# RWKV5 attention and a gated mixture of experts on one core: VectorE operands in PSUM, tables, routing and own terms divided differently

## The chip, the cores and the metric

The kernel runs on one core of a Trainium2 chip. The metric is the device time of one execution in microseconds (us). The core has a matrix engine (TensorE, PE in the profile; PEld is its weight load), three engines for elementwise work (VectorE or DVE, ScalarE or ACT, GpSimd or POOL), and SyncE (SP), which here issues loads and stores. The engines read a large on-chip memory, SBUF, with 128 partitions. TensorE writes into PSUM, a smaller memory of eight banks of 512 float32 values per partition, which the other engines can read and write too.

## The reference, cut to what matters

All values are float32. Attention has 4 batches, 8 heads, 768 positions and 48 values per head. It keeps, for every batch and head, a 48x48 state that decays by `w`; the token's own term is weighted by `u` instead:

```python
for t in range(S):
    kt, vt, rt = (k[:, :, t], v[:, :, t], r[:, :, t])
    cur = np.einsum('bhd,bhe->bhde', u[None] * kt, vt)
    y[:, :, t] = np.einsum('bhd,bhde->bhe', rt, state + cur)
    state = w[None, :, :, None] * state + np.einsum('bhd,bhe->bhde', kt, vt)
```

Its output becomes 3072 rows of 384 values. A gate picks a group of four and in it an expert of four for each row; the weight is the product of both softmax values, each with 1e-9 added to its sum. The expert is `relu(x @ w1) @ w2` with 1024 hidden values:

```python
g_idx = np.argmax(x @ w_group, axis=1)
# for the rows of group g: e_idx = argmax(xg @ w_expert[g])
h = np.maximum(xg[mask_e] @ w1[g, e], 0.0)
out[tok_idx] = (g_w * e_w)[:, None] * (h @ w2[g, e])
```

## The kernel before, in words

**Attention in chunks.** The 768 positions are cut into six chunks of 128. A chunk of one batch is a tile, `n = 4c + b`, 24 in all; two tiles make a pair `g` whose k, r and v are loaded together. With a table of powers of w by position (`T1`) and one of inverse powers (`T2`), scaled r and k (`rp`, `kp`) turn the recurrence within a chunk into matrix products. The scores of a tile (`PA`, L369) are copied below the diagonal into a matrix `am` (L373). Its diagonal is filled with the own terms `du` (sum of r·k·u, L354) by a predicated copy whose mask is the identity `id_ps` in PSUM (L380). The output `Y` is the state `R` times r (L394, from chunk 1 on) plus `am` times v (L401); the new state is `U` (L411) plus the old one, times the power of a whole chunk, `WL` (L419, L420; in chunk 0 L416 alone).

**Gate and routing.** ACT copies `Y` to `yT` (L406). A product with the gate weights `gwp` (L426), a copy `lT` (L431), and a second small product with `sel` (L447) give 20 gate values of each row, which ACT copies to `lg` (L449). `yT` is turned into rows (L436) and copied to `xt` (L441). When a chunk's four tiles are there, VectorE picks the experts (L135 to L149), PE adds up the rows already given to each expert (L153, L156), VectorE works out places and gate weights (L164 to L184), and POOL writes the rows with four indirect DMAs (L188) to the memory region of their expert. After chunk 3 (iteration 18) the two experts with most rows so far are chosen, and their weights are loaded ahead.

**The order.** One loop, `for s in range(-3, 25)`, is pipelined over tiles. Iteration s holds, in this order: the scores of tile s+1; the values of tile s, with U and R; every second time the sum `du`, for the pair of tiles s+2 and s+3, and each time the diagonal of tile s+2; the gate parts of tile s-1; the turning of k of tile s+3 (L359 on PE, L361 on ACT); the rows of tile s-1; the turning of r of tile s+3; the gate sum of tile s-1; and parts of the routing. The orders of PE, ACT, VectorE and SP are those of the program text (a manual schedule); POOL's instructions may be moved by the scheduler. Each engine takes its instructions in order, so an instruction that waits holds up what is behind it. k and r are turned through the same PSUM bank `KR`, so the transposes of r wait until ACT has copied k's. POOL makes `dg` (L337, L338), `kp` and `rp` (L348, L349), four products of 128x768 for each pair.

**Start.** Before the loop VectorE makes the powers `pw` and a reciprocal of all 512 columns, `iw` (L261). Both are transposed into `KR` and `RW` and copied to the tables by VectorE (L267). VectorE makes the first pair's `kp` (L345), POOL its `rp`. POOL clears the pads of `kp`, `rp` (L251) and the three `am` (L277). The small constants (start rows, `desc`, `bias16`, `sel`) are made by VectorE (L314 to L329) behind iotas of POOL.

**Experts.** Sixteen slots follow, in order of row counts. For each, rows are fetched (`xg`), turned, multiplied with w1 (L650) and w2 (L662), and written to the output with indirect DMAs (L674). The change does not touch them.

Of the kernel before, what the change touches and what calls it, by code (L numbers as in the profile page):

```python
# [8 lines left out]
FP32 = mybir.dt.float32  # L9
# [17 lines left out]
def kernel(  # L27
# [75 lines left out]
    WL = cst([P, HC], "WL")  # L103
# [28 lines left out]
    def route_choice(tl, L, T, sums):  # L132
# [3 lines left out]
        key = tl([P, T, NA, Eg], "key")  # L136
# [6 lines left out]
        oh = tl([P, T, NA, Eg], "oh")  # L143
        nc.vector.tensor_tensor(out=oh, in0=key, in1=spread(kx, 3, Eg), op=OP.is_equal)
        ohe = tl([P, T, G, Eg], "ohe")
        nc.vector.tensor_mul(ohe, oh[:, :, 1:NA, :], spread(oh[:, :, 0, :], 3, Eg))
        ohf = ohe.rearrange("p i g e -> p i (g e)")
        for i in range(T):
            nc.vector.tensor_add(sums[:, i + 1, :], sums[:, i, :], ohf[:, i, :])  # L149
        return mx, oh, ohe  # L150
# [10 lines left out]
    def route_place(tl, pre, ohe, T):  # L161
        ohf = ohe.rearrange("p i g e -> p i (g e)")
        at = tl([P, T, GE], "at")
        nc.vector.tensor_mul(at, pre.rearrange("p (i e) -> p i e", e=GE), ohf)  # L164
        place = tl([P, T], "place")
        nc.vector.reduce_sum(out=place, in_=at, axis=AX)
        place_i = tl([P, T], "place_i", U32)
        nc.vector.tensor_copy(place_i, place)
        return place_i

    def route_gate(tl, L, mx, oh, xt, T):
        NA = 1 + G
        ex = tl([P, T, NA, Eg], "ex")
        nc.vector.tensor_sub(ex, L, spread(mx, 3, Eg))
        nc.scalar.activation(ex, ex, AF.Exp)
        sx = tl([P, T, NA], "sx")
        nc.vector.reduce_sum(out=sx, in_=ex, axis=AX)
        nc.vector.tensor_scalar(out=sx, in0=sx, scalar1=1e-9, scalar2=None, op0=OP.add)
        gg = tl([P, T, G], "gg")
        nc.vector.tensor_mul(gg, sx[:, :, 1:NA], oh[:, :, 0, :])  # L180
        se = tl([P, T], "se")
        nc.vector.reduce_sum(out=se, in_=gg, axis=AX)
        nc.vector.tensor_mul(se, se, sx[:, :, 0])
        nc.vector.reciprocal(xt[:, :, :, Q_GATE], spread(se, 2, NQ))  # L184
# [11 lines left out]
    with ExitStack() as rec:  # L196
# [14 lines left out]
        id_ps = U[:, 256 : 256 + P]  # L211
        lT_ps = MS[:, 0:P]
        lg_ps = MS[:, P : P + NL]
        pre_ps = MS[:, 192 : 192 + B * GE]
        cnt_ps = MS[:, 192 + B * GE : 192 + B * GE + GE]

        R = [ring.tile([P, HC, D], FP32, name=f"R_{b}") for b in range(B)]
        NKP, NRP, NAM = 4, 3, 3
# [15 lines left out]
        wraw = ring.tile([P, HC], FP32, name="wraw")  # L234
        nc.vector.memset(wraw, 0.9)
        wv = w.rearrange("(hc e) d -> e d hc", e=2)
        for e, queue in enumerate((nc.sync, nc.scalar)):
            queue.dma_start(out=wraw[DP * e : DP * e + D, :], in_=wv[e])
        raw[0, "k"] = load(k, 0, "kt", 2)
        raw[0, "r"] = load(r, 0, "rt", 2)  # L240
# [9 lines left out]
        for t in kp + rp:  # L250
            nc.gpsimd.memset(t[:, :, :, D:DP], 0.0)  # L251

        pw = ring.tile([P, HC, P + 1], FP32, name="pw")
        iw = ring.tile([P, HC, P], FP32, name="iw")
        nc.vector.tensor_scalar(out=wcol, in0=wraw, scalar1=W_LEAST, scalar2=W_MOST, op0=OP.max, op1=OP.min)
        nc.vector.memset(pw[:, :, 0:1], 1.0)
        nc.vector.tensor_copy(pw[:, :, 1], wcol)
        for i in range(7):
            n = 1 << i
            nc.vector.tensor_mul(pw[:, :, 1 + n : 1 + 2 * n], pw[:, :, 1 : 1 + n], spread(pw[:, :, n], 2, n))  # L260
        nc.vector.reciprocal(iw, pw[:, :, 1 : P + 1])  # L261
        nc.vector.tensor_copy(WL, pw[:, :, P])

        def table(src, dst, bank):
            for hc in range(HC):
                nc.tensor.transpose(bank[:, hc, :], src[:, hc, 0:P], ident)
            nc.vector.tensor_copy(dst, bank.rearrange("p hc (e x) -> p (hc e) x", e=2)[:, :, 0:D])  # L267

        table(iw, T2, KR)
        table(pw, T1, RW)  # L270

        nc.vector.memset(Y, 0.0)
        nc.vector.memset(U, 0.0)
        nc.vector.tensor_copy(id_ps, ident)
        nc.vector.memset(ones, 1.0)
        for t in am:
            nc.gpsimd.memset(t, 0.0)  # L277

        nc.gpsimd.memset(gwp, 0.0)
        wg = moe_w_group.rearrange("(h d) g -> d h g", d=D)  # L280
        for m in range(2):
            rows = slice(DP * m, DP * m + D)
            nh = H - 2 * m
            nc.scalar.dma_start(out=gwp[rows, 0:nh, 0:G], in_=wg[:, 2 * m : H, :])
            for g in range(G):
                we = moe_w_expert[g].rearrange("(h d) x -> d h x", d=D)
                nc.scalar.dma_start(out=gwp[rows, 0:nh, G + Eg * g : G + Eg * (g + 1)], in_=we[:, 2 * m : H, :])

        def consts():
            nc.gpsimd.iota(iota_f, pattern=[[1, P]], base=0, channel_multiplier=0, allow_small_or_imprecise_dtypes=True)  # L290
            nc.gpsimd.iota(tok4, pattern=[[NQ * P, NCH], [NQ * S, B], [1, NQ]], base=0, channel_multiplier=NQ)
            nc.gpsimd.iota(
                region, pattern=[[RG, GE]], base=0, channel_multiplier=0, allow_small_or_imprecise_dtypes=True
            )
            for i, n in enumerate(SLOTS):
# [7 lines left out]
        FILL = ((P, P + 48), (P + 48, P + 96), (P + 96, 256))  # L303
        zeros = ring.tile([48, XW], FP32, name="zeros")
        nc.vector.memset(zeros, 0.0)

        def fill(i):
            lo, hi = FILL[i]
# [660 lines left out]
```

## Time and profile before

| what | us |
|---|---|
| median of 14 runs | 475.77 (474.52 to 477.61) |
| the profiled execution | 475.31, of it the profiled span 473.6 |
| start, to the first steady scores | 35.3 |
| chunk 0, iterations 0 to 3 | 21.2 |
| iterations 4 to 19 | 108.9 |
| last iterations, routing, first rows | 38.0 |
| experts | 270.2 |
| granted TensorE clock, mean | 0.953 |

The stages are cut at the starts of L369 for tile 1 (35.28), tile 5 (56.52) and tile 21 (165.40), and at the first product of the experts (203.38). In a line of the profile's timeline the first number is the start in us from the span's beginning and the second the duration; then come engine, line and operation, output and inputs, partitions x elements, and how many instructions the row stands for. In brackets stands how long the engine stood idle before, and what ended that. A busy engine is one that works on an instruction, even where that instruction proceeds slowly.

### The profile page before, as it was taken

To read this page: it belongs to the slowest core of one execution; us is meant where nothing else is said; L and a number is where in the kernel's file an instruction comes from. 1 tells how busy PE (TensorE), PEld (TensorE's weight loads), DVE (VectorE), ACT (ScalarE), POOL (GpSimd) and SP (SyncE) were. 2 spreads that over 40 slices of the span, in tenths; PEclk is the share of its full clock that TensorE was granted. 3 is DMA by queue.
4 is the path that set the end of the run, shared out by engine and by line. 5 is a ranking of instruction groups with operands and counts; after the bars stand their busy time and mean duration, and the time that the engine had idled before them with its cause. 6 is when DMAs were issued, how large, how long until landed. Compare 5 with 4: busy or idle time off the path is not lost.

```text
span 473.6 us, 9117 instructions
## 1 busy us (share of the span) xinstructions
PE 400.4 (85%) x3510; PEld 374.1 (79%) x3510; DVE 202.7 (43%) x377; ACT 154.4 (33%) x311; POOL 222.1 (47%) x223
## 2 busy tenths in 40 slices
PE   0359998789779896089999999999999999999990
PEld 0237877567568774079999999999999999999990
DVE  7896687998998874310121022022102211222100
ACT  0213444324334433213333423424342334144410
POOL 6798543967766303400532542452254335432444
PEclk9999999899899898579999999999999999999995
DMA  8899995647621299328698789779888988899100
GB/s 142 109 201 189 192 191 125 109 77 170 101 52 53 67 309 291 112 53 204 181 248 223 201 228 278 182 227 274 215 216 229 290 192 246 248 277 247 56 22 27
DMA packets 124018, 83.53 MB, mean 176 GB/s; under 512 B 96564, under 2 KB 115140, under 8 KB 123968
## 3 DMA queue, kind: packets, MB, share of 16 engines
q1 hardware_dynamic: 115136, 73.08, 65.8%
q0 software_dynamic: 4960, 9.55, 6.6%
q10 hardware_dynamic: 3872, 0.25, 0.6%
q8 instruction: 29, 0.48, 0.4%
q14 instruction: 21, 0.17, 0.1%
HBM read 70.11 MB, written 13.29 MB: 176 GB/s over the span
## 4 chain that ended last, share of the span: by engine, by line
issue 42%; DVE 18%; PE 18%; POOL 16%; DMA 4%; ACT 2%; POOLq 1%; DVEq 0%; ACTq 0%
POOL out_dram L674 15%; PE Y L401 4%; PE PA L369 4%; DVE R L420 3%; PE KR L359 3%; DMA out_dram<-yt,idn 3%; DVE am L380 2%; PE Y L394 2%; DVE am L373 2%; ACT kT L361 2%; PE U L411 1%; PE MS L426 1%; DVE du L354 1%; DVE key L138 1%; DVE kp L345 1%
## 5 line engine op out<-in xcount | busy, mean ns | idle before, releaser
L674 POOL DMA_INDIRECT out_dram<-yt,idn x107 | 104.1, 973 | 167.5 <-DVE yt L672 125.6
L650 PE MATMUL ph<-xe,w 128*128 128x200 f32 (+12 forms) x768 | 132.2, 332 | 9.9 <-DMA xg<-x_sorted 9.9
L650 PEld LDWEIGHTS ph<-xe,w 128*128 128x128 f32 x768 | 129.5, 192 | 10.2 <-issue 9.9
L662 PE MATMUL po<-hT,w2p 128*128 128x200 f32 (+12 forms) x768 | 130.4, 330 | 0.0
L662 PEld LDWEIGHTS po<-hT,w2p 128*128 128x128 f32 x768 | 128.1, 190 | 0.0
L671 DVE STREAM_TRANSPOSE yt<-yT 128x672 f32<-128x672 f32 (+1 forms) x16 | 13.6, 847 | 215.4 <-ACT yT L665 215.4
L655 ACT ACTIVATE hT<-ph 128x416 f32<-128x416 f32 (+12 forms) x64 | 32.0, 500 | 102.8 <-PE ph L650 102.8
L640 ACT COPY w2p<-w 128x1024 f32<-128x1024 f32 x48 | 47.1, 1048 | 9.3 <-DMA x_sorted<-xt,place_i 9.3
L188 POOL DMA_INDIRECT x_sorted<-xt,place_i x24 | 23.8, 991 | 53.2 <-ACT lg L449 18.8
L665 ACT COPY yT<-po 128x208 f32<-128x208 f32 (+12 forms) x48 | 15.6, 324 | 69.1 <-PE po L662 67.2
L373 DVE COPY_PREDICATED am<-later,PA 128x1024 f32<-128x1024 int32 x24 | 31.4, 1308 | 11.8 <-PE PA L369 11.3
L369 PE MATMUL PA<-rT,kT 48*128 48x128 f32 x384 | 30.0, 299 | 7.0 <-DVE am L373 7.0
L369 PEld LDWEIGHTS PA<-rT,kT 48*128 48x128 f32 x384 | 25.1, 200 | 8.8 <-DVE am L373 7.6
L406 ACT COPY yT<-Y 128x512 f32<-128x512 f32 x24 | 14.1, 587 | 54.7 <-PE Y L401 54.7
L380 DVE COPY_PREDICATED am<-U,du 128x1024 f32<-128x1024 int32 x24 | 31.4, 1309 | 0.4
L337 POOL TENSOR_TENSOR dg<-rt,kt 128x768 f32<-128x768 f32 x12 | 21.9, 1829 | 15.0 <-DVE du L354 15.0
L401 PE MATMUL Y<-am,vt 128*48 128x128 f32 x384 | 28.5, 295 | 0.0
L401 PEld LDWEIGHTS Y<-am,vt 128*48 128x48 f32 x384 | 21.8, 132 | 4.7 <-issue 4.1
L359 PE MATMUL KR<-ident,rp 128*128 128x128 f32 x96 | 17.0, 304 | 8.5 <-ACT kT L361 7.7
L359 PE MATMUL KR<-ident,kp 128*128 128x128 f32 x96 | 18.0, 317 | 5.7 <-DVE kp L345 5.0
L338 POOL TENSOR_TENSOR dg<-dg,ub 128x768 f32<-128x768 f32 x12 | 22.2, 1847 | 0.8
L359 PEld LDWEIGHTS KR<-ident,rp 128*128 128x128 f32 x96 | 11.1, 151 | 14.5 <-ACT kT L361 6.7
(127 smaller groups left out, 371.4 us busy)
## 6 DMA issues: line engine op xcount, KB each, us to landing
w<-in_moe_w_dram SPq DMA_DIRECT2D x64, 384.0 KB, 5.6
w<-in_moe_w_dram SPq DMA_DIRECT2D x16, 1536.0 KB, 12.2
kt<-in_k_dram SPq DMA_DIRECT2D x12, 384.0 KB, 6.1
rt<-in_r_dram SPq DMA_DIRECT2D x12, 384.0 KB, 6.3
vt<-in_v_dram SPq DMA_DIRECT2D x12, 384.0 KB, 6.4
xg<-x_sorted SPq DMA_DIRECT2D x44, 85.8 KB, 3.0
x_sorted<-zeros SPq DMA_DIRECT2D x2, 1176.0 KB
out_dram<-yt,idn POOLq DMA_INDIRECT x107, 3.3
```

The lines of the kernel that those rows point to most:

```text
L188: ins = nc.gpsimd.indirect_dma_start(out=xs_dram, out_offset=bass.IndirectOffsetOnAxis(ap=place_i[:, i : i + 1], axis=0), in_=xt[:, i].rea ...
L338: nc.gpsimd.tensor_mul(dg, dg, spread(ub, 1, 2))
L359: nc.tensor.transpose(KR[:, hc, :], two, ident)
L369: nc.tensor.matmul(PA[:, e, hc, :], lhsT=kT[rows, hc, :], rhs=rT[rows, hc, :], start=True, stop=True, skip_group_check=True,)
L373: nc.vector.copy_predicated(am[n % NAM].rearrange("p e h t -> p (e h) t"), spread(later, 1, H).bitcast(I32), PA.rearrange("p e h t -> p (e ...
L380: nc.vector.copy_predicated(am[n % NAM], spread(spread(id_ps, 1, HC), 1, 2).bitcast(I32), spread(du, 3, P))
L401: nc.tensor.matmul(Y[o : o + D, e, P * (hc // 2) : P * (hc // 2 + 1)], lhsT=vt[:, a, 2 * hc + e, :], rhs=amn[:, e, hc, :], start=(c == 0 a ...
L640: nc.scalar.copy(o4[:, kk], v4[:, kk])
L650: nc.tensor.matmul(ph[:, i, 0:n], lhsT=w1[:, ko, P * (f + i) : P * (f + i + 1)], rhs=xe[:, ko].rearrange("p i b -> p (i b)")[:, 0:n], star ...
L655: nc.scalar.activation(hTs[s][:, f : f + 2, 0:n], ph[:, :, 0:n], AF.Relu)
L662: nc.tensor.matmul(po[:, 0:n], lhsT=w2p[:, d, fo, :], rhs=hT[:, fo, 0:n], start=(fo == 0), stop=(fo == FO - 1))
L674: ins = nc.gpsimd.indirect_dma_start(out=out_q, out_offset=bass.IndirectOffsetOnAxis(ap=idn[:, i : i + 1].bitcast(U32), axis=0), in_=yt[:, ...
```

## The change

1. **Operands in PSUM.** `WL`, the routing's intermediate values and the gate values (`LG`) lie in the PSUM bank of `U`; `id_ps` moves to a bank of `Y`. Each of VectorE's operations on R and on the routing then reads or writes PSUM with one operand at least. ACT's copy `lg` is gone, and the gate sum stands ahead of the turning of r.
2. **Tables by two engines.** VectorE makes powers with the help of seven squarings (`SQ`, in PSUM) and takes reciprocals of those alone; POOL builds the inverse powers by products. Both tables go to `PA`; VectorE scales the first pair from there, and ACT copies the tables to SBUF. POOL clears no pads and no `am`; ACT does so with copies of zeros. The small constants move to POOL, the loads of the gate weights from ACT's queue to SP's. r of the first pair is loaded before k, and one of three loads of zeros into the region of rows is left out.
3. **Routing in four parts.** For chunk c, part 1 in iteration 4c+4, part 2 in 4c+5, parts 3 and 4 in 4c+6; for the last chunk all in iteration 24. The exponential is taken in part 1; the gate stands ahead of the places; two additions of 1e-9 and the cast of the places are joined to other operations, and ACT writes the token numbers once for a chunk.
4. **Own terms by two engines.** VectorE fills the diagonal for one head of each two; for the other, ACT multiplies the identity with a column of `du`, four products of 128x128. This is done for tile s+3 (before: s+2), so `du` is summed in odd iterations, and there are four `am`.

The diff, cut:

```diff
-        oh = tl([P, T, NA, Eg], "oh")
-        nc.vector.tensor_tensor(out=oh, in0=key, in1=spread(kx, 3, Eg), op=OP.is_equal)
+    def route_hot(tl, scratch, key, kx, T, sums):
+        ohg = tl([P, T, G], "ohg")
+        nc.vector.tensor_tensor(out=ohg, in0=key[:, :, 0, :], in1=spread(kx[:, :, 0], 2, G), op=OP.is_equal)
+        ohx = scratch([P, T, G, Eg], 1)
+        nc.vector.tensor_tensor(out=ohx, in0=key[:, :, 1:NA, :], in1=spread(kx[:, :, 1:NA], 3, Eg), op=OP.is_equal)
         ohe = tl([P, T, G, Eg], "ohe")
-        nc.vector.tensor_mul(ohe, oh[:, :, 1:NA, :], spread(oh[:, :, 0, :], 3, Eg))
+        nc.vector.tensor_mul(ohe, ohx, spread(ohg, 3, Eg))
+        nc.vector.tensor_mul(ohx, ohx, spread(ohg, 3, Eg))
...
-        id_ps = U[:, 256 : 256 + P]
+        WL = U[:, 192 : 192 + HC]
+        id_ps = Y[:, 0, 256 : 256 + P]
+        SQ = Y[:, 1, 256 : 256 + 8 * HC].rearrange("p (h i) -> p h i", i=8)
+        LG = U[:, 432 : 432 + B * NL].rearrange("p (i l) -> p i l", l=NL)
+        def scratch(shape, i):
+            at = (200, 280, 344)[i]
+            t = U[:, at : at + n]
...
-        NKP, NRP, NAM = 4, 3, 3
+        NKP, NRP, NAM = 4, 3, 4
...
+        def pads(t):
+            nc.scalar.copy(
+                t[:, :, :, D:DP].rearrange("p a h x -> p (a h) x"),
+                spread(zero, 1, 2 * H).to_broadcast([P, 2 * H, DP - D]),
+            )
+        def clear(t):
+            nc.scalar.copy(t.rearrange("p e h t -> p (e h t)"), zero.to_broadcast([P, H * P]))
+        pads(rp[0])
+        pads(kp[0])
+        clear(am[0])
...
-        nc.vector.reciprocal(iw, pw[:, :, 1 : P + 1])
+        for i in range(7):
+            nc.vector.tensor_mul(sq[:, :, i + 1], sq[:, :, i], sq[:, :, i])
+        nc.vector.reciprocal(rk, sq)
+        nc.vector.tensor_copy(SQ, sq)
         for i in range(7):
             n = 1 << i
+            nc.gpsimd.tensor_mul(iw[:, :, n : 2 * n], iw[:, :, 0:n], spread(rk[:, :, i], 2, n))
...
+                t1, t2 = table(pw, 0), table(iw, 1)
+                own(0)
                 for a in range(2):
-                    nc.vector.tensor_mul(kh[:, a, :, 0:D], kt[:, a], T2)
-                    nc.gpsimd.tensor_mul(rh[:, a, :, 0:D], rt[:, a], T1)
+                    nc.vector.tensor_tensor(out=rh[:, a, :, 0:D], in0=rt[:, a], in1=t1, op=OP.mult)
+                nc.scalar.copy(T1, t1)
+                for a in range(2):
+                    nc.vector.tensor_tensor(out=kh[:, a, :, 0:D], in0=kt[:, a], in1=t2, op=OP.mult)
+                nc.scalar.copy(T2, t2)
...
         def diagonal(n):
+            a4 = am[n % NAM]
             du = dus[n // 2][:, n % 2, :].rearrange("p (hc e) -> p e hc", e=2)
-            nc.vector.copy_predicated(
-                am[n % NAM], spread(spread(id_ps, 1, HC), 1, 2).bitcast(I32), spread(du, 3, P)
-            )
+            nc.vector.copy_predicated(a4[:, 0], spread(id_ps, 1, HC).bitcast(I32), spread(du[:, 0], 2, P))
+            for hc in range(HC):
+                nc.scalar.mul(a4[:, 1, hc, :], ident, du[:, 1, hc : hc + 1])
...
             if c == 0:
-                nc.vector.tensor_mul(R[b], u_up, spread(WL, 2, D))
+                nc.vector.tensor_copy(ts, u_up)
             else:
                 nc.vector.tensor_add(ts, u_up, R[b])
-                nc.vector.tensor_mul(R[b], ts, spread(WL, 2, D))
+            nc.vector.tensor_tensor(out=R[b], in0=ts, in1=spread(WL, 2, D), op=OP.mult)
...
         def gate_sum(n):
-            nc.tensor.matmul(lg_ps, lhsT=mid.pop(n), rhs=sel, start=True, stop=True, skip_group_check=True)
-            c, b = n // B, n % B
-            nc.scalar.copy(lgs[c][:, b, :], lg_ps)
+            b = n % B
+            nc.tensor.matmul(LG[:, b, :], lhsT=mid.pop(n), rhs=sel, start=True, stop=True, skip_group_check=True)
...
+        for j in range(1, NAM):
+            clear(am[j])
+        for t in rp[1:] + kp[1:]:
+            pads(t)
+        gates_in()
...
-            if 0 <= s + 2 < NT and s + 2 > 0:
-                if (s + 2) % 2 == 0:
-                    sum_own((s + 2) // 2)
-                diagonal(s + 2)
+            if 0 <= s + LA < NT:
+                if (s + LA) % 2 == 0:
+                    sum_own((s + LA) // 2)
+                diagonal(s + LA)
...
             if 0 <= s - 1 < NT:
                 rows_out(s - 1)
+                gate_sum(s - 1)
             if 0 <= s + LA < NT:
                 turn(s + LA, rps[(s + LA) // 2], "rT", 4)
-            if 0 <= s - 1 < NT:
-                gate_sum(s - 1)
...
-                if s == B * c + 4 + (0 if last else 1):
-                    route_a(c)
-                if s == B * c + 4 + (0 if last else 2):
-                    route_b(c)
-                    route_c(c)
+                at = s - (B * c + 4)
+                if at == 0:
+                    route_1(c)
...
+                if at == 1 or last and at == 0:
+                    route_2(c)
...
+                if at == 2 or last and at == 0:
+                    route_3(c)
+                if at == 2 or last and at == 0:
+                    route_4(c)
```

## The prediction

> **What bounds the kernel now.** I read the totals first, then a table of busy time by stage.
>
> ```profile
> PE 400.4 (85%) x3510; PEld 374.1 (79%) x3510; DVE 202.7 (43%) x377; ACT 154.4 (33%) x311; POOL 222.1 (47%) x223
> 56.52:165.40 108.88, 92.87 (x1396) 77.25 (x1395) 96.05 (x161) 41.14 (x101) 65.91 (x44) 0.94 0.55 107
> 203.38:473.60 270.22, 257.49 (x1536) 256.92 (x1536) 42.65 (x93) 88.61 (x157) 104.07 (x107) 0.97 0.74 199
> ```
>
> The columns after the length are PE, PEld, DVE, ACT, POOL, granted clock, DMA share. The 270 us of the experts hang on PE (95% busy), and no edit touches them. The change lives in the first 203 us: start (0 to 35.28), chunk 0 (to 56.52, 21.24), the steady part (16 iterations, 108.88) and the tail (37.98). The timeline of one even iteration, in start and duration, gives the steady chain:
>
> ```profile
> 79.73 1.16 PE L369 MATMUL PA<-rT,kT 48*128 48x128 f32 x16
> 82.59 0.59 ACT L406 COPY yT<-Y 128x512 f32<-128x512 f32 x1 [2.22 <-PE Y L401]
> 82.90 0.36 DVE L419 TENSOR_TENSOR ts<-U,R 128x192 f32<-128x192 f32 x1 [0.65 <-PE U L411]
> 83.29 5.17 DVE L420 TENSOR_TENSOR R<-ts,WL 128x192 f32<-128x192 f32 x1
> 83.33 0.27 ACT L431 COPY lT<-MS 128x128 f32<-128x128 f32 x1
> 83.83 0.59 ACT L361 COPY kT<-KR 128x512 f32<-128x512 f32 x1 [0.23 <-PE KR L359]
> 84.47 0.66 PE L359 MATMUL KR<-ident,rp 128*128 128x128 f32 x4 [0.24 <-ACT kT L361]
> 84.96 0.30 PE L447 MATMUL MS<-sel,lT 128*128 128x20 f32 x2
> ```
>
> From scores (79.73) to scores (85.19) is 5.46: PE runs through, but turning rT waits for ACT's kT copy, as both use one bank. Sixteen such periods are 87.4; 108.88 holds 21.5 more. Part of it is VectorE: R in that list took 5.17, ending with POOL's rp. A stall that costs, from the timeline:
>
> ```profile
> 113.79 5.84 DVE L420 TENSOR_TENSOR R<-ts,WL 128x192 f32<-128x192 f32 x1
> 117.58 1.82 POOL L349 TENSOR_TENSOR rp<-rt,T 128x768 f32<-128x768 f32 x1
> 119.55 0.94 DVE L354 TENSOR_REDUCE du<-dg 128x16 f32<-128x768 f32 x1
> 121.89 0.89 PE L411 MATMUL U<-vt,kp 128*48 128x48 f32 x16 [3.45 <-DVE am L380]
> ```
>
> R (both operands in SBUF) ends as POOL's run of products does; PE then stands 3.45. Grouped by shape, R's neighbour with an operand in PSUM never does so (count, then busy and mean ns):
>
> ```profile
> L420 DVE TENSOR_TENSOR R<-ts,WL 128x192 f32<-128x192 f32 x16 | 18.9, 1181 | 0.6
> L419 DVE TENSOR_TENSOR ts<-U,R 128x192 f32<-128x192 f32 x16 | 5.6, 350 | 3.8 <-PE U L411 3.8
> ```
>
> The rest is the granted clock:
>
> ```profile
> 103.18 1.16 PE L369 MATMUL PA<-rT,kT 48*128 48x128 f32 x16 [0.97 <-DVE am L373]
> 104.28 0.95 PE L394 MATMUL Y<-rT,R 48*48 48x128 f32 x16
> 105.15 1.95 PE L401 MATMUL Y<-am,vt 128*48 128x128 f32 x16
> ```
>
> L401 takes 1.08 as a rule and 1.95 here. Rows at this pace fill four stretches of 3.41 us (from 90.9, 104.5, 121.6 and 159.15), each behind one in which PE stood 1.0 to 3.3 us; such an iteration lasts 7.05 or 7.02 where 5.46 is due, 1.6 more.
>
> **The change, part by part.** *PSUM operands.* R, chunk 0's R and the routing operations get one: I price them at their undisturbed rows (R .36, L138 .24 for its mean of .86). That frees the 21.5 us, if nothing takes their place.
>
> *Own terms by two engines.* copy_predicated on 128x1024 (1.31) becomes half of it on VectorE (.65) and four 128x128 products on ACT with a column of du as the factor. No row shows such a product. Call the step from one to the next m. Nearest rows: ACT's 128x128 copy from PSUM .27; its exp on 128x80 from SBUF .27, which the slope between the 128x128 and 128x512 copies (.83 ns an element) carries to .31. Back-to-back ACT copies (kT to xt, L640) start .10 before the last one's end. So m is .17 (.27 less .10) to .31 (exp, no overlap); I take .26, between exp with overlap (.21) and without.
>
> These products stand on ACT behind yT and ahead of lT and kT. In an *even* iteration, from scores as 0: yT ends for the next start at 2.86+.48=3.34; 4m; lT .17; kT begins 3.51+4m (it was 4.10). rT's transposes follow kT by .64, the next scores those by .49, since gate_sum now stands before them (84.96 to 85.19 was .23): 4.64+4m = 5.68.
>
> In an *odd* iteration the products need the sum du of that same iteration, and VectorE comes to it only behind U, ts and R: ts 3.17+.39, R +.28 (143.51 to 143.79 in the trace), du .94: 4.78. ACT starts at 4.81; behind it queue lT, kT, xt and rT, and PE's gate_sum and rT transposes wait for those. kT at 4.98+4m, next scores at 6.11+4m = 7.15. With the second routing part, VectorE still has du to 4.78, its half .65, then ohg .21, three of .26 and four sums of .2, to 7.26; PE's prefix (L153, L156) waits for these in the same queue and ends at 7.73. Before, du was summed in even iterations, with only VectorE's own diagonal behind it.
>
> Four iterations: 5.68+7.73+5.68+7.15 = 26.24; times four 105.0; and 1.2 for PE's wait at the count of the first choice (iteration 18): 106.2 against 108.88, a gain of 2.7 (m=.21: 5.3; m=.31: a loss of .3).
>
> *Chunk 0* stalled little before (L416 .36) and has no L394; the same sums give 4.05+4m even, 5.51+4m odd, and with 6.75 for the first period (6.45 before, and .3 of the products) 6.75+6.55+5.09+6.55 = 24.94 against 21.24: loss 3.7 (3.1 to 4.5).
>
> The Trainium skill, page "ScalarE: Activation LUTs", section "What ACT_TABLE_LOAD costs", gives an ACTIVATE 186 ns plus .83 an element, some 93 more for a [128,1] pointer operand, and an overlap of 93 back to back; by it m would be about .29, an estimate, and the sum some 2.5 us later. It speaks against the change.
>
> *Start.* VectorE loses the 3.35 reciprocal, kp (3.77) and small operations of 1.7 each beside POOL; POOL gains the inverse powers, eight small constants and splits dg; ACT gains T1 and T2 (about .5 each), four clears (.95 each by L640) and twelve pads (.31). Inverse powers by about 15.6, kp 18.0, T2 18.5, three clears and the pads to 22.9, products 23.9, kT(0) 24.5 where it was 20.65; then the next tile's products wait for du: second scores 36.3 against 35.28, loss 1.0. Bounds: all of ACT's new work hidden, 2 earlier; four of POOL's small operations ahead of the inverse powers, at the .98 of a 128x384 one, 4 later.
>
> *Tail.* The copy of lg goes (.5 with its wait); the exp stands early and gate before place, so that between the last sum (186.76) and xt (189.87) the exp's trip, an addition, the cast and the token copy fall away and PE's prefix is covered: 1.5. Part 1 and 2 in one go issue a second product and the subtraction (.5), and the last own terms cost .5. Gain 1.0.
>
> *At nothing:* the ten gate-weight loads now stand on SP ahead of the second vt and the third kt and rt, issued before at 11.45, 21.0 and 21.4. Their issue took 8.8 on ACT's queue (.33+5.33+.32+2.77); behind them and a POOL clear the three come near 23.7 and land near 30, while that pair's first turn comes near 43. With those 13 us used up, each us late would be one us of the time. The dropped third zero fill, the token copy on ACT (.2 once a chunk) and the table load (moved to the start, during the first loads) lie beside DMA. A fourth am buffer frees diagonals to run three ahead.
>
> *The clock.* PE stands about 1.9 to 2.2 in every odd iteration, against 1.0 to 3.3 before the four slow stretches of the trace. One stretch with 1.1 and one with 1.3 were followed by none, so I take 8 of the 10 odd iterations with a long wait as slowing the next, at 1.2 (1.6 less what the next odd wait absorbs): 9.6. Bounds: 0 and 10 times 1.6.
>
> The Trainium skill, page "TensorE: Matmul & The Clock Gate", section "🎯 Why this matters for your kernels", warns of idle gaps over about 3 us; by it waits of 2 would cost no clock and the sum would be 476. The trace has slow rows at 104.5 behind gaps of .95, .13 and .97.
>
> **Sum**, against this run's 475.31 (span 473.6): −2.7 +3.7 +1.0 −1.0 +9.6 = +10.6: 485.9. The median of the 14 runs, 475.77, is .46 higher, well inside the range.
>
> **Rivals.** *The clock holds (other side).* One mechanism: ACT's product is short and overlapped, so PE's wait stays under 2 and no stretch drops. At m=.21 the sum is 475.31 −5.3 +3.1 +1.0 −1.0 = 473.1; with the start 2 earlier 470. It decides below m of about .24. For it: two stretches of 1.1 and 1.3 that were not followed. Against: two of the four that were had no more than 1.0 and 1.2.
> *Waits, no clock.* m of .26 to .31: 476.3 to 480.
> *It doesn't do what it says.* VectorE is held even with one operand in PSUM: the 21.5 stay on top of the new waits, 500. Against: 20 such rows (L419, L416) of which none passes .37.
> *POOL becomes the bound.* Its steady work (four products of 1.83 a pair, four scatters a chunk) is 19.7 of some 26 a chunk; a scatter that waits for a late route holds kp for the next pair by 1 to 2 us a chunk, 480 at most. Against: kp has two iterations to spare.
>
> **How the numbers follow.** Waits and clock (482 to 492) .46; waits alone (476 to 481) .17; clock holds and faster (469 to 474.5) .28; not doing what it says .06; the rest at the old time. .2% (.95 us) is about what a measurement of this kernel can tell. Faster .28, same .04, slower .68. The range, 470 to 492, takes in the three first cases; the likeliest alone is 481 to 491.
>
> **What would show it.** Right: odd iterations near 7.2 and even ones near 5.7; ACT's first product waiting for du, PE's rT transposes for kT; R at .36; L401's successor at 1.95 behind odd gaps; second scores near 36; the experts' 270 unchanged. Wrong: odd iterations under 6.5, ACT products starting before R, R still at over 1 us, or a granted clock in the steady part above .94.

## The result and the profile after

The changed kernel takes 507.69 us (median of 10 runs, 503.25 to 511.77) against 475.75 for the kernel before: a ratio of 1.064 (95% interval 1.061 to 1.068). It is slower, as forecast, but by 32 us where the prediction had 10, outside its range. Where the time went, by the same cuts as before (starts of the scores of tiles 1, 5 and 21, and the experts' first product):

| stage | before | after | difference | predicted |
|---|---|---|---|---|
| start | 35.3 | 38.8 | +3.5 | +1.0 |
| chunk 0 | 21.2 | 26.2 | +5.0 | +3.7 |
| iterations 4 to 19 | 108.9 | 129.2 | +20.3 | +6.9 (waits −2.7, clock +9.6) |
| tail | 38.0 | 40.1 | +2.1 | −1.0 |
| experts | 270.2 | 270.7 | +0.5 | 0 |
| span | 473.6 | 505.0 | +31.4 | +10.6 |

The totals of the page and the steady part in the table of stages (after the length PE, PEld, DVE, ACT, POOL, granted clock, DMA share, GB/s):

```profile
PE 424.0 (84%) x3510; PEld 390.3 (77%) x3510; DVE 151.7 (30%) x376; ACT 184.5 (37%) x402; POOL 219.6 (43%) x231
65.01:194.18 129.17, 111.01 (x1395) 90.31 (x1395) 66.94 (x157) 56.13 (x152) 61.84 (x42) 0.82 0.44 85
```

VectorE is busy 51 us less, 29 of them here (96.05 to 66.94), yet the part became longer: PE was granted .82 of its clock instead of .94, and does the same products in 111.0 us instead of 92.9. The timeline shows one odd iteration (start, duration):

```profile
90.03 1.16 PE L417 MATMUL PA<-rT,kT 48*128 48x128 f32 x16
...
93.59 0.36 DVE L470 TENSOR_TENSOR R<-ts,U 128x192 f32<-128x192 f32 x1
93.86 0.95 DVE L402 TENSOR_REDUCE du<-dg 128x16 f32<-128x768 f32 x1
94.84 1.28 ACT L431 ACTIVATE am<-ident,du 128x128 f32<-128x128 f32 x4 [1.42 <-DVE du L402]
96.03 0.24 ACT L481 COPY lT<-MS 128x128 f32<-128x128 f32 x1
96.17 0.58 ACT L409 COPY kT<-KR 128x512 f32<-128x512 f32 x1
96.33 0.40 PE L498 MATMUL U<-sel,lT 128*128 128x20 f32 x2 [1.80 <-ACT lT L481]
96.90 0.63 PE L407 MATMUL KR<-ident,rp 128*128 128x128 f32 x4 [0.17 <-ACT kT L409]
97.45 1.33 PE L417 MATMUL PA<-rT,kT 48*128 48x128 f32 x16
```

This is the predicted chain link by link: R (no longer held, .36), du, four products on ACT that had waited 1.42 for it, lT and kT behind them, PE standing 1.80; 7.42 in all. The products take .394 each, and four of them 1.28: a step of .296, between the bounds and above the .26 taken.

Cut along the clock's own stretches of 3.41 us, the same stage reads (second column PE's busy time, the third number from the end the clock):

```profile
74.40:77.81 3.41, 3.18 (x64) 2.50 (x56) 2.73 (x4) 0.59 (x1) 1.52 (x1) 1.00 0.14 28
77.81:81.23 3.42, 1.49 (x8) 1.01 (x8) 2.02 (x9) 2.99 (x9) 3.42 (x3) 1.00 1.35 212
81.23:84.64 3.41, 3.31 (x32) 2.96 (x34) 0.78 (x3) 0.00 (x0) 2.22 (x2) 0.50 0.86 110
84.64:88.05 3.41, 3.41 (x49) 2.60 (x40) 1.12 (x3) 1.06 (x3) 0.00 (x0) 0.50 0.00 0
```

PE stands 1.93 of the stretch from 77.81, and then has half its clock for two stretches, 6.8 us, although it works without a pause in them. In the profile before, each of the four spells lasted one; in a second execution of that kernel (before_here) one of three lasted two.

Times of one kernel differ between chips, and the experiments were made in four sessions (A to D in their order below), with medians of the kernel before of 488.7, 476.1, 484.2 and 477.0. So each is read by its ratio to the kernel before on the same chip. In A and C most variants have pauses behind the row writes of a chunk, in B and D they have none (see the last section), so a ratio of A or C and one of B or D compare only roughly; the changed kernel itself was run again in B alone. Of own_vector and best_one_engine only a slow execution was profiled, so of them the ratio alone is used, and their clock in the count of the last section.

### The profile page after: what moved, and what is told of

The parts are those of the page before. It is cut to its first block, busy times and chain, and to the rows that moved or that the text cites. A ratio compares the mean times of both kernels' runs of the same rounds, so it can differ in the third digit from the quotient of the medians.

```text
span 505.0 us, 9235 instructions
## 1 busy us (share of the span) xinstructions
PE 424.0 (84%) x3510; PEld 390.3 (77%) x3510; DVE 151.7 (30%) x376; ACT 184.5 (37%) x402; POOL 219.6 (43%) x231
## 4 chain that ended last, share of the span: by engine, by line
issue 40%; PE 24%; POOL 17%; ACT 8%; DVE 5%; DMA 4%; POOLq 1%; SPq 0%; ACTq 0%; DVEq 0%
POOL out_dram L741 14%; PE PA L417 7%; PE Y L450 7%; ACT am L431 4%; PE KR L407 4%; PE Y L443 3%; DMA out_dram<-yt,idn 2%; ACT kT L409 2%; DVE du L402 2%; DMA kt<-in_k_dram 1%; PE U L460 1%; ACT yT L455 1%; PE U L498 1%; DVE R L470 1%; PE MS L476 1%
## 5 line engine op out<-in xcount | busy, mean ns | idle before, releaser
L421 DVE COPY_PREDICATED am<-later,PA 128x1024 f32<-128x1024 int32 x24 | 31.4, 1309 | 57.0 <-PE PA L417 56.9
L732 ACT COPY yT<-po 128x208 f32<-128x208 f32 (+12 forms) x48 | 15.6, 324 | 69.1 <-PE po L729 67.2
L431 ACT ACTIVATE am<-ident,du 128x128 f32<-128x128 f32 x96 | 30.8, 394 | 17.7 <-DVE du L402 17.7
L417 PE MATMUL PA<-rT,kT 48*128 48x128 f32 x384 | 36.3, 343 | 0.0
L450 PE MATMUL Y<-am,vt 128*48 128x128 f32 x384 | 34.6, 339 | 0.0
L397 POOL TENSOR_TENSOR rp<-rt,T 128x768 f32<-128x768 f32 x11 | 20.0, 1814 | 32.4 <-PE KR L407 32.4
L417 PEld LDWEIGHTS PA<-rT,kT 48*128 48x128 f32 x384 | 30.7, 239 | 4.1 <-issue 3.5
L450 PEld LDWEIGHTS Y<-am,vt 128*48 128x48 f32 x384 | 26.5, 153 | 6.1 <-issue 5.3
L396 POOL TENSOR_TENSOR kp<-kt,T 128x768 f32<-128x768 f32 x11 | 20.0, 1821 | 20.0 <-PE U L460 18.4
L407 PE MATMUL KR<-ident,rp 128*128 128x128 f32 x96 | 17.7, 312 | 12.8 <-ACT kT L409 10.9
L498 PE MATMUL U<-sel,lT 128*128 128x20 f32 x48 | 9.2, 269 | 18.6 <-ACT lT L481 18.6
L498 PEld LDWEIGHTS U<-sel,lT 128*128 128x128 f32 x48 | 7.1, 188 | 22.7 <-ACT lT L481 22.5
```

The costliest lines, as they stand in the source:

```text
L407: nc.tensor.transpose(KR[:, hc, :], two, ident)
L417: nc.tensor.matmul(PA[:, e, hc, :], lhsT=kT[rows, hc, :], rhs=rT[rows, hc, :], start=True, stop=True, skip_group_check=True,)
L421: nc.vector.copy_predicated(am[n % NAM].rearrange("p e h t -> p (e h) t"), spread(later, 1, H).bitcast(I32), PA.rearrange("p e h t -> p (e ...
L431: nc.scalar.mul(a4[:, 1, hc, :], ident, du[:, 1, hc : hc + 1])
L450: nc.tensor.matmul(Y[o : o + D, e, P * (hc // 2) : P * (hc // 2 + 1)], lhsT=vt[:, a, 2 * hc + e, :], rhs=amn[:, e, hc, :], start=(c == 0 a ...
L498: nc.tensor.matmul(LG[:, b, :], lhsT=mid.pop(n), rhs=sel, start=True, stop=True, skip_group_check=True)
```

## The experiments

| kernel | session | ratio to before | 95% interval | steady part, us |
|---|---|---|---|---|
| changed, unchanged copy | B | 1.070 | 1.066 to 1.074 | 122.9 |
| own_vector | A | 1.018 | 1.006 to 1.030 | |
| products_last | A | 1.018 | 1.009 to 1.027 | 126.6 |
| filler | A | 1.053 | 1.045 to 1.062 | 127.8 |
| du_early | A | 1.007 | 1.003 to 1.011 | 116.0 |
| du_prefix | B | 0.979 | 0.976 to 0.982 | 98.8 |
| start_fix | B | 1.054 | 1.052 to 1.057 | 129.9 |
| before_wl | C | 0.996 | 0.994 to 0.999 | 111.9 |
| best_two_engines | C | 0.966 | 0.962 to 0.970 | 106.8 |
| best_one_engine | C | 0.962 | 0.955 to 0.970 | |
| filler_again | C | 1.049 | 1.042 to 1.056 | 126.0 |
| lg_apart | D | 1.039 | 1.035 to 1.043 | 119.6 |
| du_start | D | 0.973 | 0.969 to 0.976 | 100.8 |
| last_du | D | 0.950 | 0.944 to 0.956 | 94.9 |

**The controls.** The kernel before and the changed one, run again beside others.

> The kernel before, unchanged, as a control: a profile on the same chip as the runs beside it. If the pauses of 2 to 4 us that stood in the last runs behind the row writes of a chunk (POOL's indirect DMAs) belong to the chip and not to the variants, they show here too, and the steady part is longer than 108.9; if not, it is 107 to 111.

> The changed kernel, unchanged, as a control on the same chip: 1.06 to 1.07 of the time before, steady part 127 to 133, slow stretches of the clock of 3.4 or 6.8 us behind nearly every stretch in which PE stood more than 1 us.

Before: steady part 110.4, with slow spells and no pause behind row writes; changed: 1.070 and 122.9, a little under the expected 127 to 133. The profiled execution was the fastest of its four (500.0 against a median of 508.4). The finding stands on another chip. The steady part of the changed copy, to be held against du_prefix below:

```profile
65.57:188.42 122.85, 104.10 (x1396) 84.64 (x1395) 66.99 (x157) 56.24 (x152) 62.19 (x42) 0.87 0.46 89
```

Outside the spells of half clock its iterations last 5.84 (even), 7.35 (odd) and 8.61 (odd, with the second routing part).

**Own terms back on VectorE.**

```diff
-            nc.vector.copy_predicated(a4[:, 0], spread(id_ps, 1, HC).bitcast(I32), spread(du[:, 0], 2, P))
-            for hc in range(HC):
-                nc.scalar.mul(a4[:, 1, hc, :], ident, du[:, 1, hc : hc + 1])
+            nc.vector.copy_predicated(a4, spread(spread(id_ps, 1, HC), 1, 2).bitcast(I32), spread(du, 3, P))
```

> The changed kernel with the whole diagonal filled by VectorE again (one predicated copy of 128x1024, no product on ACT); all else stays as changed. Theory A (ACT's four products stand ahead of lT and kT and in odd iterations wait for du; PE then stands 1.8 us behind kT and the clock drops to half for the following even iteration): odd iterations without routing fall from 7.4 to about 5.5, even ones from 8.1 to about 5.5, and the 129.2 us of the steady part to 90 to 100 (the iterations with the second routing part still wait for PE's prefix); time 465 to 478. Rival B (the routing operations and PSUM sharing of U are what PE waits for): steady part above 118, time above 495.

**The products later on ACT.**

```diff
+        def products(n):
...
                 turn(s + LA, rps[(s + LA) // 2], "rT", 4)
+                products(s + LA)
```

> The changed kernel with ACT's four products moved behind the copy of rT, at the end of ACT's list of an iteration; VectorE still does its half. Theory A: the products' work (1.28 us an iteration) is not the cost, only where they stand is, so the steady part falls to 90 to 100 and the time to 465 to 478, as with the products taken away. Rival C (ACT has become too full, whatever the order): yT of the next tile comes late, the steady part stays above 115 and the time above 490.

Both came out at 1.018, from 1.064 to 1.070 for the changed kernel on other chips, so as far as intervals of 1% can tell the place of the products is worth as much as the products themselves: theory C, a full ACT, falls. Chunk 0 went from 26.2 to 20.5 with them last, and its undisturbed iterations take 4.73 to 4.85. But both missed the times of theory A (465 to 478; the runs lie at 494 to 504), about where the rivals B and C had them, and the expected 90 to 100 of the steady part was missed by 27 us: the iterations with the second routing part still took 7.4, spells of half clock still followed them, and the iterations behind the row writes had become 9.4 to 10.1. So the wait for du was not the only one that drops the clock, and rival B's routing has a part in it (du_prefix and lg_apart show which). Against filler, the next kernel, on the same chip, products_last is 16 us shorter in the profile, 9 of it in the start and chunk 0 and only 1.2 in the steady part.

**A filler on PE, no wait taken away.** In odd iterations, ahead of the gate sum:

```diff
+                if s % 2 == 1 and s + LA < NT:
+                    for i in range(10):
+                        nc.tensor.transpose(PA[:, 0, i % HC, :], ident, ident)
                 gate_sum(s - 1)
```

> The changed kernel with ten extra transposes of the identity on PE ahead of the gate sum in odd iterations (into the bank of the scores, which is free then; some 1.6 us, about as long as PE's wait there); no wait is taken away. Theory A with the clock: PE no longer stands still, so the clock holds: slow products (1.95 us for the score-times-v group) vanish behind these iterations, even iterations fall from 8.1 to about 5.9, odd ones stay at 7.3, the steady part falls to 108 to 116, time 487 to 495. Rival D (even iterations are long by a wait of their own, and the slow products are something else): no change or longer, 507 or more.

> The changed kernel with ten extra transposes ahead of the gate sum in odd iterations once more, on a chip without the pauses behind the row writes: the clock's price by itself, since no wait is taken away. Theory A: even iterations 5.85 instead of 7.3 to 9.1, odd ones as before at 7.3 (8.6 with the second routing part), steady part 109 to 114, time 10 to 15 us below the changed kernel's 508, ratio to before 1.03 to 1.05. If the clock costs little: ratio 1.06 to 1.07 as without.

The mechanism showed, the total did not follow as expected (steady part 127.8 and 126.0; in A the time even met rival D's 507 or more). The granted clock in the steady part rose from .82 (.87 in the copy) to .92 and .93: 6 and 5 stretches of half clock instead of 14 and 9. Even iterations fell to 5.84 wherever no such spell lay in them (four and three of the eight), and odd ones with the second routing part stayed at 8.6. But the other odd ones, 7.35 to 7.5 in the changed kernel, took 9.2 and in the last chunk 10.9 in A, 7.8 to 9.1 and 10.7 in C: pauses behind the row writes, in which VectorE took up U 7.1 and 5.1 us late in all. The ratio fell only from 1.064 to 1.053 and 1.049. Whether the filler itself lengthens these pauses is not shown, as the changed kernel was not run in A or C.

**du one iteration earlier, then the prefix one later.**

```diff
-                if (s + LA) % 2 == 0:
-                    sum_own((s + LA) // 2)
+                if s == -LA:
+                    sum_own(0)
+                if (s + LA) % 2 == 1 and s + LA + 1 < NT:
+                    sum_own((s + LA + 1) // 2)
                 diagonal(s + LA)
```

> The changed kernel with the sum du moved one iteration earlier, into even iterations, so that ACT's products have their column when they come up; they still stand ahead of lT and kT. Theory A: odd iterations become like even ones, 5.8 to 6.0 (yT, four starts of .30, lT, kT), PE's wait falls from 1.8 to some .4, fewer slow stretches; steady part 98 to 110, time 473 to 488. If the products' length alone costs (theory C of a full ACT): no change, above 500.

and besides that `route_prefix(pre_ps, ohe, sums(c), B)` moved from `route_2` to the head of `route_3`:

> The changed kernel with du summed one iteration earlier, and also PE's prefix (L160, L163) moved from the iteration of the second routing part to the next, ahead of the gate and the places, so that PE no longer waits for VectorE's one-hot products. Theory A: the iterations of part two fall from 7.15 to 5.85, no slow stretch is left in the steady part but behind the row writes, steady part 97 to 107, time .96 to .99 of before. Rival E (PE's prefix is not what drops the clock, or the wait appears at the places): steady part 112 to 118 as with du early alone, time 1.0 to 1.01 of before.

With du early the odd iterations without routing are 5.84 and 5.91, like the even ones, where no pause stands in them (two of four), and the ratio falls to 1.007 in a session with pauses; the expected 98 to 110 and 473 to 488 were missed (116.0 and 492.9). With the prefix moved as well the kernel is faster than before, .979, and on one chip with the copy of the changed kernel 465.8 against 508.4. Its steady part, in the table of stages:

```profile
59.06:157.89 98.83, 91.16 (x1396) 74.21 (x1395) 65.65 (x157) 55.29 (x152) 63.47 (x43) 0.98 0.61 118
```

The clock is .98, with a single slow stretch. The iterations with part two went from 7.14 to 5.9 (once 6.97), the next one from 5.84 to 6.23, since the prefix now takes PE's time there: the prefix by itself is worth some .8 a chunk and the spells of slow clock. Sessions A and B differ, so the step from 1.007 to .979 holds the pauses too.

**The start.**

```diff
         clear(am[0])
+        for j in range(1, NAM):
+            clear(am[j])
+        for t in rp[1:] + kp[1:]:
+            pads(t)
...
-                    nc.gpsimd.tensor_mul(dg[:, a], rt[:, a], kt[:, a])
-                    nc.gpsimd.tensor_mul(dg[:, a], dg[:, a], ub)
+                    nc.vector.tensor_mul(dg[:, a], rt[:, a], kt[:, a])
+                    nc.vector.tensor_mul(dg[:, a], dg[:, a], ub)
...
```

In the changed kernel's timeline POOL's first dg product waits for k, and the inverse powers behind it are ready at 16.43; then ACT clears three am and five pads before the first kT copy:

```profile
9.41 0.99 POOL L377 TENSOR_TENSOR dg<-rt,kt 128x384 f32<-128x384 f32 x1 [3.22 <-DMA kt<-in_k_dram]
...
15.80 0.63 POOL L311 TENSOR_TENSOR iw<-iw,rk 128x256 f32<-128x256 f32 x1
...
20.68 2.94 ACT L287 COPY am<-zero 128x1024 f32<-128x1024 f32 x3
...
26.23 0.57 ACT L409 COPY kT<-KR 128x512 f32<-128x512 f32 x1
```

> The changed kernel with ACT's clears of the other three am and the five other pads moved ahead of the table copies (ACT stands idle there from 4.9 to 18.7), and the first pair's dg made by VectorE, which is idle too, so that POOL's inverse powers do not stand behind it. If these two are the start's loss (the product chain of POOL held by dg waiting for k, 7 us; the clears 4.4 us ahead of the first kT copy): first scores at 20 to 25 instead of 31.5, second scores at 27 to 32 instead of 38.8, time 7 to 11 us below the changed kernel's. If the loads or POOL's other work hold the first pairs anyway: first scores earlier, tile 5's (65.0) by under 3.

(The clears and pads are taken out behind the tables, in the part not shown.) First scores came at 24.7, second at 32.1 instead of 38.8, tile 5 at 59.4 instead of 65.6; the median fell by 6.0 (508.4 to 502.4), a little under the 7 to 11 expected.

**One part alone on the kernel before.**

```diff
-                nc.vector.tensor_mul(R[b], ts, spread(WL, 2, D))
+                nc.vector.tensor_mul(R[b], ts, spread(WLp, 2, D))
```

with `WLp` a copy of `WL` beside U in PSUM.

> The kernel before with one thing of the change alone: R's second operand, the chunk's power, is read from PSUM (a copy beside U) from chunk 1 on; routing, own terms, start and order stay as before. If VectorE's holds come from POOL's use of SBUF beside an operation with both operands there: R falls from a mean of 1.18 to .36, the pauses of PE behind it go with most slow stretches of the clock, steady part 95 to 102 instead of 108.9 to 110.4, time .97 to .985 of before. If an operand in PSUM does not help (rival of the prediction): R stays over 1 us, time unchanged.

Half right. Its R does fall to .354, so an operand in PSUM does end the hold; but the time falls by .4% only, not 1.5 to 3%. The timeline shows the hold on the next operations that have both operands in SBUF:

```profile
101.09 1.80 POOL L350 TENSOR_TENSOR kp<-kt,T 128x768 f32<-128x768 f32 x1
101.25 3.85 DVE L149 TENSOR_TENSOR cum<-cum,ohe 128x16 f32<-128x16 f32 x4
...
102.85 1.80 POOL L351 TENSOR_TENSOR rp<-rt,T 128x768 f32<-128x768 f32 x1
104.94 0.69 PE L156 MATMUL MS<-cum,ones 128*128 128x64 f32 x2 [2.71 <-DVE cum L149]
```

The four sums (.17 each in the kernel before) last 3.85: the first two take 1.68 and 1.72 and end as POOL's kp and rp do. PE waits 2.71, and the clock halves. So part of the hold moved from R to the routing: 3.0 us to these sums and 1.4 to L137, of the 13 that R lost. The other routing rows are held as they were before (L138 1.02, here .99), and the steady part, 111.9, is no shorter; what kept the rest of R's 13 us from showing was not taken apart. The change ends the hold on all of these operations.

**Gate values in another bank.**

```diff
-        LG = U[:, 432 : 432 + B * NL].rearrange("p (i l) -> p i l", l=NL)
+        LG = MS[:, 272 : 272 + B * NL].rearrange("p (i l) -> p i l", l=NL)
```

The changed kernel's timeline, second routing part:

```profile
111.08 0.40 PE L498 MATMUL U<-sel,lT 128*128 128x20 f32 x2 [1.80 <-ACT lT L481]
...
111.52 0.17 DVE L147 TENSOR_TENSOR ohg<-U,kx 128x16 f32<-128x16 f32 x1 [1.12 <-PE U L498]
...
113.04 0.69 PE L163 MATMUL MS<-cum,ones 128*128 128x64 f32 x2
```

VectorE's first one-hot is held 1.12 by PE's gate sum, which writes other columns of the same bank.

> The changed kernel with the gate values in another PSUM bank (that of the gate parts) than the routing's intermediate values and U; nothing else. Theory F: VectorE's first one-hot (L147) waits some 1.1 us for PE's gate sum only because both touch one bank, and PE's prefix behind it with it. Then L147's wait for L498 goes, the iterations with the second routing part shorten by .7 to 1.1 at an equal clock (from 8.6 at the full clock to 7.6 to 7.9), time 2 to 6 us below the changed kernel, ratio to before 1.05 to 1.065. If the one-hots wait for something else too: no change in the wait of L160, ratio 1.064 to 1.07.

Its first one-hot, in the timeline:

```profile
78.28 0.16 DVE L147 TENSOR_TENSOR ohg<-U,kx 128x16 f32<-128x16 f32 x1
```

L147 no longer waits for PE at all; the iterations with part two take 7.74 at full clock, and the ratio falls to 1.039, more than expected. The tail is 36.6, and the clock granted over a whole run is .93 in the median, .915 in the changed kernel's runs; that the shorter wait alone spares the slow spells is not shown.

**All repairs.**

> The changed kernel with three repairs together: ACT's products behind the copy of rT, PE's prefix one iteration later, and the start's clears and pads ahead of the table copies with dg of the first pair on VectorE; own terms by two engines, du in odd iterations as changed. Theory A: periods near 5.35 in the steady part (it was 5.84 with the products ahead of kT), 86 to 92 in all, no slow stretch in it or one, second scores at 28 to 29; time .935 to .955 of before. If ACT is too full or du still holds something: periods stay at 5.8 or above, time .96 or more.

> The same three repairs with the own terms by VectorE alone (no products on ACT): tells what dividing them is worth by itself. If VectorE has room without the holds (67 us busy of 129 in the steady part): the same time as with two engines within .5%. If VectorE's half of .65 an iteration is needed for the routing parts: 2 to 6 us longer.

> The changed kernel with du one iteration earlier, PE's prefix one later, and the start repaired (clears, pads, dg of the first pair on VectorE); ACT's products still ahead of lT and kT. If the repairs add: the .979 of the first two and some 6 us of the start, .962 to .97 of before, periods 5.84 to 5.95.

> The same with ACT's products behind the copy of rT as well. Theory A: periods 5.35 to 5.45 instead of 5.85, steady part 8 shorter than the kernel beside it, unless the pauses behind the row writes stand in it; ratio .945 to .96. If the periods of 5.85 hide the row writes and 5.35 do not: the same ratio as beside it, with longer iterations behind the row writes.

The two "best" kernels are equal within their intervals (.966 and .962): dividing the own terms between the engines makes no difference that can be told once the holds are gone. The .935 to .955 was missed; in session C iterations of 8.7 to 9.8 stand behind the row writes. In session D du_start lies just above its range (.973): VectorE's early du found POOL late once (by 4.1), and chunk 0 took 25.4. Moving the products behind rT (last_du) gives 5.32 to 5.38 instead of 5.84, a steady part 5.9 shorter (8 expected) and .950, 451 us against 477: the fastest kernel of the study. Its even iteration, by the timeline:

```profile
48.75 1.16 PE L421 MATMUL PA<-rT,kT 48*128 48x128 f32 x16
48.86 0.58 ACT L413 COPY rT<-KR 128x512 f32<-128x512 f32 x1 [0.42 <-PE KR L411]
49.34 1.28 ACT L439 ACTIVATE am<-ident,du 128x128 f32<-128x128 f32 x4
...
52.84 0.59 ACT L413 COPY kT<-KR 128x512 f32<-128x512 f32 x1 [0.24 <-PE KR L411]
53.48 0.66 PE L411 MATMUL KR<-ident,rp 128*128 128x128 f32 x4
54.07 1.16 PE L421 MATMUL PA<-rT,kT 48*128 48x128 f32 x16
```

The products now lie in ACT's pause before yT, and kT is copied as soon as PE has turned it. One iteration of last_du lasts 11.98, where POOL has become the one waited for:

```profile
79.54 0.95 DVE L406 TENSOR_REDUCE du<-dg 128x16 f32<-128x768 f32 x1 [5.08 <-POOL dg L385]
81.19 1.11 PE L451 MATMUL Y<-rT,R 48*48 48x128 f32 x16 [4.16 <-DVE am L433]
```

## Why the prediction was wrong

- **Direction and main chain: right.** The wait of ACT's products for du, the queue of lT, kT and rT behind them and PE's stand were as described. With the measured step of .296 its sums give 5.82 and 7.29; at full clock 5.84 and 7.35 were measured. That the waits are the cause is shown on one chip: with the waits for du and for the prefix taken away (du_prefix) the changed kernel's 1.070 became .979 and its steady part 98.8 instead of 122.9. How this divides between the two is less sure, as moving the products (1.018) and du alone (1.007) were run on a chip with pauses. The bounds at m=.21 and m=.31 were summed a little wrong: its own terms give gains of 5.1 and .3 where it has a gain of 5.3 and a loss of .3; nothing hangs on it.
- **The clock: the term that failed most.** The step "8 of the 10 odd iterations with a long wait as slowing the next, at 1.2" became 2.05 for each of eight even iterations, and 1.0 more in the odd ones. At full clock the steady part would be four times (2 x 5.84 + 7.35 + 8.61) and the 1.2 at the count, 111.8; measured 129.2, so 17.4 for the clock instead of 9.6, and more than the upper bound of 16 (in the copy's profile, with 122.9, 11.1). The even iterations average 8.04, with .15 of it for the count, in place of 5.84. The prediction took the price from spells that last one stretch; behind the new waits they mostly last two (six of the eight in the steady part). Why two, the runs don't settle.
- **The second routing part: a wait overlooked.** "to 7.26 ... ends at 7.73" took VectorE to go straight on to the one-hots. At full clock it was 8.61, since the one-hot waits for the gate sum in the shared bank (lg_apart: 7.74). Four times .88 here, 3.5, and the longer product in the other twelve iterations (5.84 for 5.68, 7.35 for 7.15), 2.1, turn the waits' −2.7 into +2.9.
- **"That frees the 21.5 us, if nothing takes their place": the holds went, and the new waits took their place.** In the changed kernel R is at .354 and the routing's row of L138, L137 there, at .25, as priced. With the waits repaired the steady part is 98.8 (du_prefix) and 94.9 (last_du), 10 and 14 of the 21.5; last_du has one iteration of 11.98 in it, 6.6 above its neighbours. R by itself is worth .4% (before_wl).
- **Start: right chain, mis-sized.** Predicted 36.3 for the second scores, measured 38.8: inverse powers at 16.4 rather than 15.6, the first kT at 26.2 rather than 24.5, and that of tile 2, at 37.1, behind du as foreseen. start_fix shows that 6 us of it can be had back.
- **Chunk 0:** 3.7 forecast, 5.0 measured: .4 from the longer step, .4 from a spell of half clock at its end (7.22 against 6.83 in filler), the rest is open. **Tail:** −1.0 forecast, +2.1 measured; it begins with a spell of half clock (.71 granted, .78 before). In lg_apart and du_prefix, where none stands at its start, it is 36.6 and 36.0, 1.4 to 2 below before, so without the spell its own edits give what was forecast or more.
- **Rivals.** "The clock holds" and "waits, no clock" are refuted; "it doesn't do what it says" too, as R is at .354 in all variants; POOL as the bound appeared only after the repairs.
- **The step and the gaps by the Trainium skill.** The estimate of about .29 from its page "ScalarE: Activation LUTs", section "What ACT_TABLE_LOAD costs", met the .296 measured, so here the page was better than the row chosen, for some 2 us. Its page "TensorE: Matmul & The Clock Gate", section "🎯 Why this matters for your kernels", asks for no idle gaps over some 3 us; here a gap of 1.80 (up to 96.33) was followed by half clock from 98.31 on, and the trace decides.

## What to carry to other kernels

Before a helper engine takes over a piece of work, look at what stands behind that piece in its queue and when the piece's input is ready: the same four products cost some 3 to 6% ahead of a copy on the matmul chain, and nothing that could be told behind it. Where PE is nearly the bound, as here, a wait of one or two microseconds can cost its length and, by the clock, about as much again in the iteration after it. Values of two engines that need not meet should not share a PSUM bank, and a hold between VectorE and POOL is best ended for all neighbours, or part of it moves to the next.

## What the runs showed of the hardware

**When the clock halves.** In the first 175 us of the 17 profiles, cut along the clock's stretches of 3.41 us, 545 stretches ran at full clock. Where PE stood under .7 us of it, 1 of 402 was followed by half clock; .7 to 1.0, 4 of 53; 1.0 to under 1.6, 18 of 35; 1.6 or more, 50 of 55 (a row or two at the borders can fall either way). Spells last one or two stretches, and in two cases three. The Trainium skill's page "TensorE: Matmul & The Clock Gate", section "HAM oscillation — how this bites in real kernels", puts the drop behind idle gaps over some 3.4 us; here PE idle for a third to a half of a stretch was often enough, and the runs decide.

**A bank as a lock.** The 1.12 us wait of L147 joins two engines that touch different columns of one bank; the Trainium skill's page "PSUM — Partial Sum Buffer", section "PSUM bank collisions raise a hardware error", asks for just such a guard by bank, and lg_apart shows its price here: 8.61 to 7.74 for the iteration, 1.039 instead of 1.064 to 1.070 for the kernel (on different chips).

**Pauses behind row writes.** In sessions A and C VectorE, ACT and SP took up PE's results 1.2 to 4 us late while a chunk's rows were written, in this case of filler_again (timeline) by 1.8:

```profile
119.47 0.53 PE L460 MATMUL U<-vt,kp 128*48 128x48 f32 x16
...
121.80 0.37 SPq L250 DMA_DIRECT2D vt<-in_v_dram  x1
121.81 0.36 DVE L469 TENSOR_TENSOR ts<-U,R 128x192 f32<-128x192 f32 x1 [2.40 <-PE RW L486]
```

The load that needs vt free and VectorE's ts, which needs U, start together, 1.8 after U's products should have ended. In after_here, du_prefix and lg_apart, on other chips, the same places show nothing of the kind. But before_wl, in C too, has nothing over 1.4, so it is not the chip alone. What holds the results there was not settled.
